# Attention recurrence, expert mixture and gated FFN on one core: the whole recurrence in a written order, experts after it, two blocks per expert, routing in two halves of twelve tiles

## The chip, the cores and the metric

One core of a Trainium2 chip runs the whole program in one launch. The metric is the device time of one execution in microseconds (us). Engines are named as the profile names them: PE is TensorE's matmuls, PEld its weight loads, DVE VectorE, ACT ScalarE, POOL GpSimd, SP SyncE (which here issues DMAs).

## The reference

Three stages follow one another. In the code below the names are those of the reference, cut to what is computed.

```python
# 1. gated linear attention: 4 batches, 8 heads, 768 steps, head dimension 48
f = 1 / (1 + exp(-f_logit))
for t in range(768):
    state = f[:, :, t, :, None] * state + k[:, :, t] (outer) v[:, :, t]
    y[:, :, t] = q[:, :, t] @ state
x = y as (3072 tokens, 384)
# 2. mixture of experts: 8 experts, width 1024, two per token
noisy = x @ w_gate + log1p(exp(x @ w_noise)) * noise
top2, weights = two largest of noisy per token, softmax over the two
out[token] += weight * (relu(x[token] @ w1[e]) @ w2[e])
# 3. gated FFN, width 1536
xn = out / sqrt(mean(out**2) + 1e-6) * rms_g
result = (silu(xn @ w_gate2) * (xn @ w_val2)) @ w_out2
```

## The kernel before

**Recurrence.** The 768 steps of a batch are cut into 6 chunks of 128 tokens, which gives 24 chunks (NT) for the four batches; a chunk holds all eight heads. Chunk n goes through a row of helpers: clip, gates and sums turn the gate logits into running sums, prep makes the scaled keys KT and queries QT from them, keys turns KT around on PE, scores multiplies KT by QT (16 small matmuls) and masks them into AM, inter multiplies QT by the state Ss, state makes the chunk's own contribution from Ks and Vs, carry adds it to the state (su on DVE, then Ss on POOL), attend multiplies AM by Vs, and rows (one chunk later) turns the result to token rows, writes them to DRAM (xd) and makes the logits for routing (lg). The loop over chunks in gla_stream calls these helpers; chunk i's iteration also does parts of the chunks i+1 to i+5.

**Routing.** router is a generator of steps: top-2 of a set of tiles, a prefix count (PE), slot numbers, one-hot tables, and at the end a list of token rows for each expert. It runs twice: over the first NTA = 8 tiles while the recurrence runs (ahead), and over the other 16 as jobs among the first expert units (rest). After the second, experts are ranked by their count, and the late blocks go by rank.

**Experts.** An expert's tokens are cut into blocks. The first block of each expert holds CAPA = 256 rows from the first NTA tiles; then each rank has two late blocks, of 256 rows and of what CAPS leaves (256 to 348 rows). A block has 8 units of 128 hidden columns. A unit is a first product (l1: 3 slices of the input, three matmuls each), a relu that splits the result into hhi (ACT) and hlo (DVE), and, two units later, a second product (l2: three matmuls per tile of 128 rows). Every operand is split in a high and a low half, so a product is three matmuls: the function three. Block rows are gathered by GpSimd DMAs (fetch), turned on DVE and split (turn).

**Weights.** They come as 768 KB loads on SP's queue (raw), and each holds two parts. take_part makes one part ready: ACT copies its high half (whi), another engine subtracts (wlo). FFN weights (wide parts) also need the integer operations cv on DVE. A part goes to a spot that has come free, starts the next load if there is room, and take_part is called once per unit; among the expert units a wide part is let through only every third unit (rest).

**Order.** PE's order is as written throughout. In the recurrence up to chunk 14 (FETCH + 3) the order of ACT, DVE and POOL is as written too (manual_schedule(ALL)); afterwards a scheduler sets theirs. From chunk 14 on, the driver behind gla_stream takes turns between the recurrence and expert_stream by their costs (debt), so that expert products stand between the recurrence's matmuls on PE, with PSUM banks as SHARED gives them. expert_stream runs over all units of all blocks: 192 expert units, then 6 FFN blocks of 512 tokens with 12 units each.

**FFN.** A unit multiplies by gate and val (18 matmuls of 512 columns), makes sg on ACT and DVE, splits to hhi and hlo, and multiplies by out (12 matmuls of 384 columns). Its inputs are gathered, combined, normalized and turned by steps attached to the units ahead.

## Time and profile before

| | us |
|---|---|
| median of 3 runs | 1117.58 (1116.81 to 1119.4) |
| the profiled execution, whole | 1115.89 |
| its span | 1114.1 |
| recurrence, with the first half of routing | 0 to 111.5 |
| block 0 is turned | 111.5 to 118 |
| mix of recurrence and first experts | 118 to 200.3 |
| experts with the second half of routing, then experts alone | 200.3 to 345, 345 to 641 |
| FFN | 641 to 1114.1 |

The rows from the profile have these columns. A stretch: its length, then the busy us and the instructions of each engine, the granted clock of PE as a share of the full one, the busy share of the DMA engines and GB/s. A group of instructions: line, engine, operation, the tiles it writes and reads, partitions x elements, count, then busy us and mean ns of one, then the idle time of the engine just before and what ended it. A timeline row: start, length, engine, line, operation, tiles, and in brackets the idle time before and its releaser. Matmuls are pipelined, so the length of one is longer than the distance to the next.

### The profile page before, as it was taken

How to read it: one execution, taken by the hardware profiler on the slowest of the kernel's cores; microseconds unless marked ns; L12 is line 12 of the kernel's file. 1: busy time of each engine (PE TensorE's matmuls, PEld its weight loads, DVE VectorE, ACT ScalarE, POOL GpSimd, SP SyncE). 2: the span in 40 equal slices, each digit the busy share in tenths (PEclk: the TensorE clock that was granted, in tenths of full speed). 3: DMA queues.
4: the chain of work that ended last, by engine and by line, in shares of the span. 5: the costliest groups of instructions: out<-in, count | busy, mean ns of one | idle time of the engine just before them, and what ended most of it. 6: DMA issues, size and time to landing. Idle time of an engine off the chain costs nothing. (4 is left out here: it accounts for less than half of the span.)

```text
span 1114.1 us, 18967 instructions
## 1 busy us (share of the span) xinstructions
PE 1054.8 (95%) x7057; PEld 959.4 (86%) x7057; DVE 684.8 (61%) x1463; ACT 486.9 (44%) x1100; POOL 385.1 (35%) x417
## 2 busy tenths in 40 slices
PE   5988799978889999999999999899999999999997
PEld 4877699868889999999998988788888888888886
DVE  6899775699777654565666769735345444353332
ACT  5675664545556543454554545423223223232211
POOL 2257544567674344444636443120030020110000
PEclk7987899999999999999999999999999999999999
DMA  9986444456667533444443444020020110110000
GB/s 307 296 264 217 133 156 138 136 173 202 216 211 230 184 106 104 150 142 128 156 147 121 150 129 137 33 71 15 1 85 1 37 49 1 57 29 1 29 1 31
DMA packets 87992, 132.97 MB, mean 119 GB/s; under 512 B 8719, under 2 KB 63907, under 8 KB 87891
## 3 DMA queue, kind: packets, MB, share of 16 engines
q1 hardware_dynamic: 78323, 112.25, 31.0%
q0 software_dynamic: 9568, 19.43, 6.2%
q8 instruction: 57, 0.93, 0.3%
q14 instruction: 44, 0.36, 0.1%
HBM read 107.63 MB, written 24.02 MB: 118 GB/s over the span
## 5 line engine op out<-in xcount | busy, mean ns | idle before, releaser
L655 PE MATMUL bank<-xhi,whi 128*128 128x256 f32 (+8 forms) x1008 | 340.4, 338 | 22.6 <-DVE hlo L760 14.6
L655 PE MATMUL bank<-xlo,whi 128*128 128x256 f32 (+8 forms) x1008 | 336.4, 334 | 1.2 <-DVE xlo L643 1.2
L655 PE MATMUL bank<-xhi,wlo 128*128 128x256 f32 (+8 forms) x1008 | 336.2, 333 | 0.0
L655 PE MATMUL bank<-whi,hhi 128*128 128x384 f32 (+2 forms) x728 | 247.2, 340 | 5.9 <-ACT y L776 5.9
L655 PE MATMUL bank<-whi,hlo 128*128 128x384 f32 (+2 forms) x728 | 246.0, 338 | 0.0
L655 PE MATMUL bank<-wlo,hhi 128*128 128x384 f32 (+2 forms) x728 | 245.3, 337 | 0.0
L655 PEld LDWEIGHTS bank<-xhi,whi 128*128 128x128 f32 x1008 | 191.6, 190 | 48.4 <-DVE hlo L760 17.7
L655 PEld LDWEIGHTS bank<-xlo,whi 128*128 128x128 f32 x1008 | 191.6, 190 | 17.9 <-DVE xlo L643 2.4
L655 PEld LDWEIGHTS bank<-xhi,wlo 128*128 128x128 f32 x1008 | 191.6, 190 | 17.4
L731 POOL DMA_INDIRECT xg<-xd,stokr x139 | 135.1, 972 | 141.8 <-ACT hhi L759 113.9
L760 DVE SCALAR_TENSOR_TENSOR hlo<-bank,hhi 128x256 fp32r<-128x256 f32 (+7 forms) x192 | 82.8, 432 | 110.2 <-ACT hhi L759 109.7
L210 ACT ACTIVATE whi<-raw 128x256 fp32r<-128x256 f32 (+1 forms) x320 | 127.0, 452 | 46.0 <-DMA raw<-in_moe_w_dram 37.8
L212 DVE TENSOR_TENSOR wlo<-raw,whi 128x256 fp32r<-128x256 f32 (+1 forms) x246 | 131.4, 566 | 22.7 <-ACT whi L210 22.2
L655 PEld LDWEIGHTS bank<-whi,hhi 128*128 128x128 f32 (+2 forms) x728 | 133.6, 184 | 10.1 <-ACT y L776 6.5
L655 PEld LDWEIGHTS bank<-wlo,hhi 128*128 128x128 f32 (+2 forms) x728 | 133.5, 183 | 6.2
L655 PEld LDWEIGHTS bank<-whi,hlo 128*128 128x128 f32 (+2 forms) x728 | 133.0, 183 | 3.4
L759 ACT ACTIVATE hhi<-bank 128x256 fp32r<-128x256 f32 (+7 forms) x192 | 74.8, 390 | 133.9 <-PE bank L655 131.2
L801 POOL DMA_INDIRECT xg<-yd,slots x40 | 44.0, 1100 | 243.1 <-ACT hhi L853 207.5
L850 DVE TENSOR_TENSOR sg<-bank,sg 128x512 f32<-128x512 f32 x72 | 49.7, 690 | 119.6 <-ACT sg L849 119.6
L849 ACT ACTIVATE sg<-bank 128x512 f32<-128x512 f32 x72 | 43.2, 600 | 145.4 <-PE bank L655 145.4
L853 ACT ACTIVATE hhi<-sg 128x512 fp32r<-128x512 f32 x72 | 45.4, 631 | 116.2 <-DVE sg L851 116.0
L212 POOL TENSOR_TENSOR wlo<-raw,whi 128x384 fp32r<-128x384 f32 (+1 forms) x74 | 69.5, 946 | 54.6 <-ACT whi L210 46.1
(159 smaller groups left out, 1141.3 us busy)
## 6 DMA issues: line engine op xcount, KB each, us to landing
raw<-in_moe_w_dram SPq DMA_DIRECT2D x64, 768.0 KB
Qs<-in_kq_dram SPq DMA_DIRECT2D x11, 1024.0 KB
yd<-y SPq DMA_DIRECT2D x48, 192.0 KB
Fs<-in_f_logit_dram SPq DMA_DIRECT2D x11, 512.0 KB
Vs<-in_v_dram SPq DMA_DIRECT2D x24, 192.0 KB
xd<-x SPq DMA_DIRECT2D x24, 192.0 KB
raw<-in_moe_w_gate_dram SPq DMA_DIRECT2D x6, 768.0 KB
raw<-in_moe_w_val_dram SPq DMA_DIRECT2D x6, 768.0 KB
```

What stands on the lines that cost most here:

```text
L210: nc.scalar.activation(hi[:, j], raw[:, j], AF.Copy)
L212: e.tensor_tensor(lo[:, j], raw[:, j], hi[:, j].bitcast(F32), op=OP.subtract)
L655: nc.tensor.matmul(o, a, b, start=start and i == 0, stop=stop and i == 2)
L731: paced(nc.gpsimd.indirect_dma_start(out=b.xg[i][:, k_], out_offset=None, in_=table, in_offset=bass.IndirectOffsetOnAxis(ap=rows_of[:, k_, ...
L759: mark[0] = nc.scalar.activation(hhi[:, :N], p[:, :N], AF.Relu).ins
L760: mark[1] = nc.vector.scalar_tensor_tensor(hlo[:, :N], p[:, :N], 0.0, hhi[:, :N].bitcast(F32), op0=OP.max, op1=OP.subtract).ins
L801: paced(nc.gpsimd.indirect_dma_start(out=y, out_offset=None, in_=ya if n < GROUP else yd, in_offset=bass.IndirectOffsetOnAxis(ap=at_, axis ...
L849: nc.scalar.activation(sg, ps[0], AF.Sigmoid)
L850: nc.vector.tensor_tensor(sg, ps[0], sg, op=OP.mult)
L853: mark[0] = nc.scalar.activation(hhi, sg, AF.Copy).ins
```

## The change

The recurrence, all 24 chunks, goes into the written order for all engines, and the experts start when it is over. The loop body no longer yields costs; SHARED, the debt and RATIO go. In chunk 0 the warm-up matmuls (warm) grow by 6, 4 and 6, and its attend comes before the gates of later chunks. From the sixth chunk on, clip is a Relu with bias on ACT instead of a max on DVE, and gates takes the shift back in its bias. The second operation of carry goes from POOL to DVE, and so do all wlo subtractions of expert weights that POOL had. The first routing half has 12 tiles in chunks 12 to 20, the gathers of block 0 are spread over chunks 20 to 24, and its three turns come after the recurrence. The first expert loads start at chunks 14 and 16 (2 and 4 before); take_part runs in chunks 20 to 23 (6 to 11 before).

CAPA is 384, and each rank has one late block with the rest (384 to 476 rows), so 128 expert units where 192 were. A gather has no wait on carry any more (st["C"]), up to two gathers are placed at a unit, and a block's turns are placed at 5 to 2 units ahead. In every fourth unit take_part is called twice. Input tiles are 512 wide for all blocks, and a block's second y goes through DVE in the first blocks too.

```diff
-    NTA = 8
+    NTA = 12
     GROUP = 4
-    CAPA = 256
+    CAPA = 384
...
     def constants():
         nc.vector.memset(ones, 1.0)
+        nc.vector.memset(shift, GATES_MAX + 1.5)
...
             else:
                 for j in range(shape[1]):
                     nc.scalar.activation(hi[:, j], raw[:, j], AF.Copy)
-                    e = nc.vector if banks[0] is not BANK and (j or self.late) else nc.gpsimd
-                    e.tensor_tensor(lo[:, j], raw[:, j], hi[:, j].bitcast(F32), op=OP.subtract)
+                    nc.vector.tensor_tensor(lo[:, j], raw[:, j], hi[:, j].bitcast(F32), op=OP.subtract)
...
-    def clip(n, s=slice(0, HP)):
+    def clip(n, s=slice(0, HP), scalar=True):
         f = st["f", n][:, s]
-        nc.vector.tensor_scalar(f, f, -GATES_MAX - 1.5, None, op0=OP.max)
+        st["shift", n] = scalar
+        if scalar:
+            nc.scalar.activation(f, f, AF.Relu, bias=shift)
+        else:
+            nc.vector.tensor_scalar(f, f, -GATES_MAX - 1.5, None, op0=OP.max)
     def gates(n, s=slice(0, HP)):
...
-        nc.scalar.activation(l, f, AF.Exp, scale=-1.0)
+        nc.scalar.activation(l, f, AF.Exp, scale=-1.0, bias=shift if st["shift", n] else 0.0)
...
             nc.vector.tensor_tensor(t, u, Ss[c % 2][:, :, :D], op=OP.add)
-            st["C"] = nc.gpsimd.tensor_tensor(sn, t, w, op=OP.mult).ins
+            nc.vector.tensor_tensor(sn, t, w, op=OP.mult)
...
-            with tc.issue_after(st["C"]):
-                paced(nc.gpsimd.indirect_dma_start(
+            paced(nc.gpsimd.indirect_dma_start(
...
-            with behind(), tc.high_priority(0 if banks[0] is not SHARED else 50):
+            with behind():
                 nc.vector.transpose(t[:, :, :n],
...
-                if i % 2 and t0:
+                if i % 2:
                     nc.vector.tensor_copy(y[:r], b.acc[i][:r])
...
     for r, most in enumerate(CAPS):
-        blocks += [moe_block(r, CAPA // P, 256, E + r),
-                   moe_block(r, CAPA // P + 2, most - CAPA - 256, E + r)]
+        blocks += [moe_block(r, CAPA // P, most - CAPA, E + r)]
...
-        if i < E:
-            where = (-4, -3)
-        elif i < NM:
-            where = (-5, -3, -2)
+        if i < NM:
+            where = (-5, -4, -3, -2)
...
-        while room.get(at_unit, 0) > (at_unit % 3 == 0):
+        while room.get(at_unit, 0) > 1:
...
             take_part(g_)
+            if g_ % 4 == 1:
+                take_part(g_)
...
-        for i in range(NT + 3):
-            es = ExitStack()
-            if i < FETCH + 3:
-                es.enter_context(tc.manual_schedule(engines=ALL))
...
+            for i in range(NT + 2):
...
+                if valid(i):
+                    scores(i)
+                safe()
+                if i == 0:
+                    warm(6)
+                    run(prep, 1)
...
+                if i == 0:
+                    warm(4)
+                if valid(i):
+                    state(i)
+                    carry(i)
+                    if i == 0:
+                        attend(i)
+                if i == 0:
+                    warm(6)
+                    run(decay, 2)
+                    clip(3, scalar=False)
+                    gates(3)
...
+                if i in (14, 16):
+                    start_loads()
...
+                if 20 <= i < 24:
+                    take_part(0)
...
+    plan = {12: [idle, step, step], 13: [idle, step], 14: [step, step], 15: [step], 16: [step],
+            17: [step], 18: [step], 19: [idle, step], 20: [step]}
+    for i, fn in enumerate([fn for fns in blocks[0].fetches for fn in fns]):
+        plan.setdefault(20 + (i + 1) // 3, []).append(fn)
...
-    recurrence, experts = gla_stream(), expert_stream()
-    debt, begun = 0.0, 0
-    for cost in recurrence:
...
+    gla_stream()
     gla.close()
...
+    for fn in blocks[0].turns:
+        fn()
...
-    for gap in (0, 0, 0, 0, 0, 1, 0, 0, 0, 0, 0, 0, 0, 0, 2, 1, 2, 2):
+    for gap in (0, 0, 0, 0, 1, 0, 0, 0, 0, 0, 0, 2, 1, 2, 2):
         jobs += [step] + [idle] * gap
```

Three places show how instructions stand on their engines. The first is VectorE in the recurrence: one chunk from one AM to the next, while no routing runs. AM is the masked scores, KT and QT the scaled keys and queries, lg the logits, su and Ss the state's carry, cs the gates' running sums, Fs the clipped logits. Before:

```order
L394 TENSOR_TENSOR AM<-scores,mask 128x1024
L364 SCALAR_TENSOR_TENSOR KT<-Ek,Qs_136 128x512
L456 TENSOR_REDUCE lg<-bank_789 128x16
L369 TENSOR_TENSOR QT<-cs,Qs_136 128x512
L418 TENSOR_TENSOR su<-bank_809,Ss_131 128x192
L342 SCALAR_TENSOR_TENSOR cs<-chain,L 128x512
L328 TENSOR_SCALAR Fs_132<-Fs_132 128x4x128
```

After, the same stretch:

```order
L395 TENSOR_TENSOR AM<-scores,mask 128x1024
L365 SCALAR_TENSOR_TENSOR KT<-Ek,Qs_138 128x512
L457 TENSOR_REDUCE lg<-bank_845 128x16
L370 TENSOR_TENSOR QT<-cs,Qs_138 128x512
L419 TENSOR_TENSOR su<-bank_865,Ss_131 128x192
L420 TENSOR_TENSOR Ss_132<-su,cs 128x4x48
L343 SCALAR_TENSOR_TENSOR cs<-chain,L 128x512
```

The clip (L328) has gone from VectorE, and the second operation of the carry (L420, to Ss) has come, right behind su.

The second place is TensorE at the end of the recurrence. Before, the rows around one chunk's scores, with the experts' first products (xhi, whi) and second products (whi, hhi) between the recurrence's matmuls:

```order
L655 MATMUL bank_1670<-whi_1044,hhi 128x384
L655 MATMUL bank_1670<-wlo_1045,hhi 128x384
L655 MATMUL bank_1670<-whi_1044,hlo 128x384
L430 MATMUL bank_1728<-QT,Ss_130 64x128 x8
L405 MATMUL bank_1739<-Vs_126,Ks_124 64x48 x8
L440 MATMUL bank_1728<-AM,Vs_126 64x128 x8
L390 MATMUL scores<-QT,KT 128x128 x8
L655 MATMUL bank_1795<-xhi_1465,whi_1159 128x256
L655 MATMUL bank_1795<-xlo_1466,whi_1159 128x256
L655 MATMUL bank_1795<-xhi_1465,wlo_1160 128x256
```

After, the last two chunks and what follows:

```order
L391 MATMUL scores<-QT,KT 128x128 x8
L453 MATMUL bank_1934<-columns,yT 128x112 x4
L431 MATMUL bank_1943<-QT,Ss_131 64x128 x8
L406 MATMUL bank_1953<-Vs_129,Ks_125 64x48 x8
L441 MATMUL bank_1943<-AM,Vs_129 64x128 x8
L391 MATMUL scores<-QT,KT 128x128 x8
L453 MATMUL bank_1995<-columns,yT 128x112 x4
L431 MATMUL bank_2004<-QT,Ss_132 64x128 x8
L441 MATMUL bank_2004<-AM,Vs_130 64x128 x8
L453 MATMUL bank_2034<-columns,yT 128x112 x4
L656 MATMUL bank_2078<-xhi,whi_1835 128x384
L656 MATMUL bank_2078<-xlo,whi_1835 128x384
```

No expert matmul stands before the last rows (L453) any more, and the first one is that of a block with 384 rows.

The third place is VectorE at the first units of the FFN. sg and hlo belong to the units, cv to FFN weights. Before:

```order
L850 TENSOR_TENSOR sg<-bank_8341,sg 128x512
L851 TENSOR_TENSOR sg<-bank_8351,sg 128x512
L854 TENSOR_TENSOR hlo<-sg,hhi 128x512
L850 TENSOR_TENSOR sg<-bank_8375,sg 128x512
L851 TENSOR_TENSOR sg<-bank_8385,sg 128x512
L774 COPY y<-bank_8174 128x384
L854 TENSOR_TENSOR hlo<-sg,hhi 128x512
L850 TENSOR_TENSOR sg<-bank_8419,sg 128x512
L851 TENSOR_TENSOR sg<-bank_8429,sg 128x512
```

After:

```order
L849 TENSOR_TENSOR sg<-bank_7303,sg 128x512
L850 TENSOR_TENSOR sg<-bank_7313,sg 128x512
L853 TENSOR_TENSOR hlo<-sg,hhi 128x512
L178 TENSOR_SCALAR cv<-cv 128x384 x2
L179 SCALAR_TENSOR_TENSOR cv<-raw,cv 128x384 x2
L181 SCALAR_TENSOR_TENSOR cv<-raw,cv 128x384 x2
L849 TENSOR_TENSOR sg<-bank_7356,sg 128x512
L850 TENSOR_TENSOR sg<-bank_7366,sg 128x512
L773 COPY y<-bank_7112 128x384
L853 TENSOR_TENSOR hlo<-sg,hhi 128x512
```

Between the first and the second FFN unit there is now the conversion of a weight part (cv), where none stood; counted over the whole engine, 5 of the 18 FFN parts are converted ahead of the first FFN unit, 10 before.

## Rows read from the trace of the kernel before

**Rows 1.** Stretches: us, busy us (and count) of each engine, PEclk, DMA, GB/s.

```profile
33.00:66.00 33.00, 33.00 (x490) 29.14 (x488) 29.86 (x45) 25.32 (x53) 11.99 (x17) 1.00 0.91 301
66.00:98.00 32.00, 24.44 (x254) 20.93 (x253) 30.56 (x81) 18.09 (x40) 16.37 (x17) 0.68 0.59 181
111.50:118.00 6.50, 0.89 (x16) 0.69 (x14) 5.13 (x8) 3.94 (x8) 2.07 (x3) 0.74 0.49 170
118.00:200.30 82.30, 80.66 (x859) 73.89 (x859) 55.96 (x96) 46.64 (x107) 39.19 (x48) 0.96 0.42 136
200.30:345.00 144.70, 125.32 (x878) 119.18 (x877) 119.37 (x287) 79.13 (x217) 95.13 (x96) 0.98 0.62 199
345.00:641.00 296.00, 292.90 (x1968) 280.91 (x1967) 181.82 (x440) 142.45 (x367) 139.69 (x137) 1.00 0.45 142
```

**Rows 2.** Timeline of TensorE, recurrence alone, 37 to 67 us.

```profile
37.15 1.16 PE L390 MATMUL scores<-QT,KT 48*128 48x128 f32 x16
...
63.24 1.09 PE L430 MATMUL bank<-QT,Ss 48*64 48x128 f32 x16
...
65.75 1.16 PE L390 MATMUL scores<-QT,KT 48*128 48x128 f32 x16
```

**Rows 3.** TensorE's groups by form, the mix, 118 to 200.3 us.

```profile
L655 PE MATMUL bank<-xhi,whi 128*128 128x256 f32 x51 | 16.6, 326 | 6.8 <-ACT xhi L642 5.6 <-DVE hlo L760 1.1
...
L655 PE MATMUL bank<-whi,hhi 128*128 128x384 f32 x30 | 11.2, 374 | 0.0
```

**Rows 4.** Timeline of TensorE among the experts, 377 to 381 us.

```profile
377.78 0.28 PE L655 MATMUL bank<-xhi,whi 128*128 128x256 f32 x1
...
378.85 0.34 PE L655 MATMUL bank<-whi,hhi 128*128 128x384 f32 x1
...
379.90 0.28 PE L655 MATMUL bank<-xhi,whi 128*128 128x256 f32 x1
```

**Rows 5.** Timeline of TensorE while eight tiles are routed, 66 to 98 us.

```profile
77.14 1.97 PE L430 MATMUL bank<-QT,Ss 48*64 48x128 f32 x16 [0.27 <-POOL Ss L419]
...
84.72 1.89 PE L452 MATMUL bank<-columns,yT 128*128 128x112 f32 x8
...
96.11 1.86 PE L390 MATMUL scores<-QT,KT 48*128 48x128 f32 x16
```

**Rows 6.** VectorE's groups by form, recurrence alone, 30 to 66 us.

```profile
L328 DVE TENSOR_SCALAR Fs<-Fs 128x512 f32<-128x512 f32 x7 | 4.4, 624 | 0.0
...
L418 DVE TENSOR_TENSOR su<-bank,Ss 128x192 f32<-128x192 f32 x5 | 1.8, 352 | 2.3 <-PE bank L405 2.3
```

**Rows 7.** Waits, 200.3 to 345 us: engine, waited for, total us, times, longest.

```profile
ACT whi L210 <- DMA raw<-in_moe_w_dram: 35.1, 21, 3.5
...
PE bank L655 <- DVE hlo L760: 13.4, 12, 2.0
```

**Rows 8.** The page's costliest groups: the experts' subtractions on GpSimd.

```profile
L212 POOL TENSOR_TENSOR wlo<-raw,whi 128x384 fp32r<-128x384 f32 (+1 forms) x74 | 69.5, 946 | 54.6 <-ACT whi L210 46.1
```

**Rows 9.** Timelines of GpSimd, VectorE and TensorE, FFN's first block, 658 to 701 us.

```profile
671.99 1.85 POOL L207 TENSOR_TENSOR wlo<-cv,whi 128x768 fp32r<-128x768 f32 x1 [2.82 <-ACT whi L206]
...
659.98 0.69 DVE L854 TENSOR_TENSOR hlo<-sg,hhi 128x512 fp32r<-128x512 f32 x1 [0.70 <-ACT hhi L853]
...
663.49 0.68 DVE L850 TENSOR_TENSOR sg<-bank,sg 128x512 f32<-128x512 f32 x1
...
672.65 1.73 DVE L854 TENSOR_TENSOR hlo<-sg,hhi 128x512 fp32r<-128x512 f32 x1 [0.70 <-ACT hhi L853]
...
691.77 0.67 DVE L850 TENSOR_TENSOR sg<-bank,sg 128x512 f32<-128x512 f32 x1
...
700.29 0.33 PE L173 MATMUL bank<-ident,xm 128*128 128x128 f32 x1 [2.28 <-ACT xm L824]
```

**Rows 10.** VectorE's groups by form, whole span: FFN weight slices.

```profile
L182 DVE SCALAR_TENSOR_TENSOR cv<-raw,cv 128x256 int32<-128x256 int32 x36 | 14.5, 415 | 0.1
```

**Rows 11.** Timeline of SyncE's DMA issues, 205 to 260 us.

```profile
205.22 20.39 SPq L256 DMA_DIRECT2D raw<-in_moe_w_dram  x4
```

## What I expect of the change, and how it is worked out

> **What bounds the kernel now.** I read the table of stretches first [rows 1]: from 345 to 641 us TensorE is busy for 292.9 of 296 us at the full clock, so that stage can only change through the matmuls themselves. The loss lies ahead of it. From 66 to 98 us TensorE is busy 24.4 of 32 us at a mean granted clock of 0.68 while VectorE is busy 30.6; from 200.3 to 345 us TensorE stands still for 19 us and VectorE is busy 119 of 145. From 33 to 66 us the recurrence runs alone with TensorE at 33.0 of 33 us: alone, and undisturbed, it is bound by TensorE, not by its chain. Its pace: six chunks (one head sequence) from the scores at 37.15 to those at 65.75, 28.6 us, or 4.77 a chunk [rows 2]. Mixing expert work into it can therefore fill nothing in such a stretch. From 118 to 200.3 the mix is nearly dense (80.7 of 82.3), but it holds one product after the other: 17 units of the first product and 15 of the second (51 and 30 matmuls of each kind, three and two a unit) [rows 3].
>
> A unit of 256 rows takes 1.07 us for nine 256-column matmuls and 1.05 for six 384-column ones [rows 4]: 119 and 175 ns each, 0.44 ns a further column. So by 200.3 us the old kernel has the whole recurrence and 17 x 1.07 + 15 x 1.05 = 33.9 us of expert work. Without the latter it stands at 166.4: that is what the new order has to beat.
>
> **The change, part by part.**
>
> *Recurrence alone.* Start: the fourth scores stand at 37.15 us before [rows 2]; three chunks of 4.77 are 14.3, so 22.9 us are start. The warm-up matmuls in chunk 0 stand where TensorE waits, and chunk 0's attend comes ahead of the next chunks' gates; what they can give is the low clock of the first two chunks. At the low level sixteen matmuls of a chunk take 1.97 us where 1.09 stands at the full one [rows 2, 5]. I take 6 us, between 0 and 9: fourth scores at 31.2. Then 21 chunks at 4.77, 100.2: 131.4 without routing.
>
> The clip moves from VectorE (0.62 us a chunk) to ScalarE, and the second operation of the carry comes from GpSimd to VectorE (I take the 0.35 of its neighbour of the same width) [rows 6]. VectorE is busy 29.9 us in 33, or 6.9 chunks: 4.3 a chunk, then 4.3 - 0.62 + 0.35 = 4.05. ScalarE goes from 25.3/6.9 = 3.7 to about 4.3 [rows 1]. Both stay under 4.77, so these two cost nothing while TensorE is the cover; if that went, VectorE's 4.05 would be the floor, not a loss.
>
> *First routing half, now 12 tiles, in chunks 12 to 20.* Eight tiles cost this: scores at 65.75 and 96.11 [rows 2, 5] are three chunks in 30.4 us, 16 more than 14.3. In the stretch VectorE's 30.6 less three chunks (13) leaves 17.6, of which the two wlo operations are 2 and the rest routing, slowed by GpSimd. For 12 tiles, half more of what goes by tiles and no GpSimd beside it: 17. Spread over nine chunks, VectorE needs 9 x 4.05 + 17 = 53.5 against TensorE's 43: 10.5 more. To that come the clock and the ordered waits of TensorE on routing results: the matmuls at 77.14 to 86.61 stand back to back, and all are at the low level [rows 5]. Two such chunks cost 2 x 3.8; I take 17 more in all, between 8 and 35. The recurrence ends at 148 and 1.5 us for the last rows: 150.
>
> The Trainium skill (TensorE: Matmul & The Clock Gate, "What's actually happening") says that the clock is held low by default and activity releases it. By that, chunks without gaps would come back at once, and the 17 would be 10.5. The row disagrees: 9.5 us of back-to-back matmuls, still low. The sum goes by the row.
>
> *Turning block 0.* Before, TensorE works 0.9 of 6.5 us at 111.5 to 118 [rows 1]. Now three tiles instead of two, but the first one's transpose stands inside chunk 21 in VectorE's order. Same 6 us, plus 1.5 for a slow first unit: the experts begin at 157.5, against 166.4. Gain 9.
>
> *Blocks.* First products: early 64 units of 9 x 175 ns + 9 x 175 = 3.15 us, 201.6. Late: 3348 columns over the eight experts, a block's mean of 418 columns takes 8 x 119 + 0.44 x 1300 = 1.52 us over the eight, x 9 matmuls x 8 units = 109.7; second products, 31 row tiles x 3 x 175 ns x 8 = 130. In all 441. Before, 128 units of 2.12, then 77 + 97: 445. Row tiles are the same number (7 an expert, 6 for the last), so only 576 matmuls less: gain 4.
>
> *Standing still in the experts.* Before: 641 - 200.3 = 440.7, less the 445 - 34 = 411 of products and 1.5 of routing: 28 us. Its waits are TensorE on hlo (13.4 us), behind ScalarE waiting for weights (35.1 us) [rows 7]: both are in-order engines, and a unit of 2.1 us wanted a part of weights each. Now a unit is 3.15 us for one part, the double-buffered bank of the first product leaves 4.7 us instead of 3.2, routing has 12 tiles for 16, and the 74 subtractions of GpSimd (69.5 us) [rows 8] go to VectorE, which is faster at them when GpSimd is silent: beside the GpSimd subtraction at 671.99, the same VectorE operation takes 1.73 us, and 0.69 without [rows 9]. VectorE in the first 24 units (75 us): hlo 0.5, parts 1.25 x 1.0, turns 0.45 a unit, which is 2.2 x 24 = 53, and 19 of routing: 72. That is close to full, so I leave 12 us (4 to 28). Four late row tiles on three y buffers are in that. Gain 16.
>
> *FFN weights.* Late blocks of the new kernel are 64 units for the same 64 parts, where 128 units were; a wide part is let through only every third unit. VectorE's order has 5 of the 18 FFN parts ahead of the first FFN unit, and 10 before. Thirteen are left for the first FFN block. A gate or val part is three slices with three operations each, the dearer of 0.415 us [rows 10], so 2.6 to 3.7. Before, with one part a unit, the sg operations at 663.49 and 691.77 are four units apart: 7.07 us a unit, where TensorE needs 18 x 0.23 (512 columns, 0.44 ns each above 119) + 12 x 0.175 = 6.2; the debt came due as 2.3 us ahead of the transposes at 700.29 [rows 9]. Five more parts are 13 to 18 us more for VectorE, of which about half found slack at 641 to 666. I add 8 (0 to 20). Rest of the FFN (before 1114.1 - 641 = 473) unchanged: 481.
>
> *Sum.* 157.5 + 441 + 1.5 + 12 + 481 = 1093 of span, 21 to 22 less than 1114.1. The profiled execution took 1115.9, the median is 1117.6; so 1117.6 - 21.6 = 1096.
>
> **Rivals.**
>
> *A. The expert stage keeps its waits.* Loads came some 5 us apart while ScalarE waited for them (four in 20.4 us on SP's queue [rows 11]), and the new kernel, taking 1.25 parts a unit, asks for one each 5.0 us until its 18 slots are full. If the 28 us stay: 1112. For it: the 35 us of waits. Against it: the surplus quarter isn't needed by the product, one part a unit is.
>
> *B. The clock stays low from chunk 12 on (slower).* Nothing but the recurrence is on TensorE, and each wait on routing can drop it. A low chunk is 4.77 x 1.97/1.09 or about 8.6 us. Twelve low chunks cost 46 and hide the 17 of routing: 1096 + 29 = 1125. It decides from about ten low chunks on. For it: the mean clock of 0.68 from 66 to 98. Against it: by 98 the clock was back, with chunks as dense as before. [...]
>
> *C. The FFN's weights come late.* The last val part is taken one unit ahead of its use; if each of the last five stops TensorE, 20 us rather than 8: 1108.
>
> *D. It is better than that.* The clock recovers, routing costs only VectorE's 10, the expert stage waits 4 us: 1096 - 7 - 8 - 3 = 1078.
>
> **How the numbers follow.** Forecast 0.55 (own range 1083 to 1107), A 0.15, B 0.12, C 0.08, D 0.10. The likeliest is 1096. For 8 in 10 the range reaches D's middle and A and C: low 1075, high 1119; B beyond it stays out. Measurement can tell about 0.2% (2.2 us), so faster is below 1115.3: all of D, nearly all of the forecast, most of C and three quarters of A, 0.82. Same 0.05, out of A and B's edge; slower 0.13, B and the far ends of A and C.
>
> **What would show it.** Right: scores 4.8 us apart in chunks 2 to 11; VectorE close to full in chunks 12 to 20 and 55 to 65 us there; the first 384-column matmul of block 0 at 150 to 165; standing still under 15 us from there to the FFN; first FFN matmul about 610; over 5 us more lost in the first FFN block than before. Wrong: chunks above 5.5 us without routing (then the chain, not TensorE, bounds the recurrence alone), the clock low past chunk 20, TensorE still waiting on hlo for 20 us among the early experts, or a FFN block 0 that costs nothing more.

## The result and the profile after

The changed kernel takes 1106.02 us (median of 4 runs, 1105.08 to 1109.45) against 1118.49 for the kernel before on the same chip: a ratio of 0.9893, interval 0.9865 to 0.9922. It is 12.5 us faster; the forecast was 21.6 faster, at 1096, in a range of 1075 to 1119. Beside later experiments it was run again, unaltered (e5 below): 1096.41 against 1116.47, 0.9828 (0.9802 to 0.9855). Both values are results. Between the two profiles lie 10.9 us of span, and 7.5 of them come from the stall described below.

The profile of the first (its execution took 1109.45, its span is 1107.7), in stretches, with the columns of [rows 1]: recurrence alone, routing, two places of standing still, the experts with the second routing half, the experts alone, and the first FFN block.

```profile
36.46:83.40 46.94, 46.94 (x690) 41.57 (x689) 41.76 (x63) 41.23 (x77) 2.67 (x10) 1.00 0.81 265
83.40:133.80 50.40, 41.57 (x616) 35.98 (x614) 48.39 (x124) 33.66 (x64) 4.23 (x8) 1.00 0.44 140
138.00:149.00 11.00, 4.46 (x35) 3.04 (x32) 2.42 (x6) 0.81 (x3) 8.29 (x9) 0.66 0.20 55
161.70:166.50 4.80, 0.08 (x2) 0.04 (x1) 3.08 (x7) 1.95 (x4) 0.00 (x0) 0.88 0.68 203
166.50:345.00 178.50, 174.81 (x997) 170.86 (x998) 130.54 (x358) 97.01 (x250) 88.89 (x85) 0.97 0.62 201
345.00:619.10 274.10, 272.30 (x1514) 257.43 (x1513) 162.18 (x378) 129.21 (x314) 121.45 (x119) 1.00 0.49 154
619.10:715.80 96.70, 82.91 (x369) 70.25 (x368) 77.71 (x169) 47.88 (x106) 35.52 (x21) 0.91 0.36 113
```

What to read here, row by row. Alone, the recurrence is TensorE without a gap, as in the first of [rows 1]. While 12 tiles are routed, VectorE is busy 48.39 of 50.40 us and the clock is full (1.00; 0.68 in the second of [rows 1]). In the third row TensorE works 4.46 of 11 us and nothing but GpSimd is busy: a stall that the trace of before has nothing like. The experts wait far less (175 of 178.5, where [rows 1] have 125 of 145). The last row, the first FFN block, is 96.7 us long with VectorE busy 78; before it was 79.2, from its first 512-column matmul at 643.89 to that of the second block.

The waits tell the same. TensorE waits 0.8 us for hlo among the first experts, 166.5 to 345 us, where it was 13.4 us in [rows 7]. ScalarE still waits 28.9 us for weights, where it was 35.1:

```profile
ACT whi L208 <- DMA raw<-in_moe_w_dram: 28.9, 18, 3.7
...
PE bank L656 <- DVE hlo L759: 0.8, 2, 0.4
```

And in the first FFN block, 619 to 716 us, a wait that before had none of:

```profile
POOL wlo L205 <- ACT whi L204: 51.4, 12, 11.1
ACT whi L204 <- DVE cv L181: 26.8, 22, 3.1
...
PE bank L656 <- POOL wlo L205: 10.6, 3, 3.8
```

Read from the bottom up it is a chain: TensorE waits for an FFN part's low half on GpSimd, GpSimd for ScalarE's high half, ScalarE for VectorE's cv.

The stall at chunk 22, in TensorE's timeline, 136 to 162 us:

```profile
137.38 0.67 PE L406 MATMUL bank<-Vs,Ks 128*64 128x48 f32 x16
137.88 0.43 PE L441 MATMUL bank<-AM,Vs 128*64 128x128 f32 x4
...
139.36 0.44 PE L441 MATMUL bank<-AM,Vs 128*64 128x128 f32 x4 [0.34 <-issue]
...
141.64 2.04 PE L391 MATMUL scores<-QT,KT 48*128 48x128 f32 x10 [0.17 <-issue]
148.84 2.05 PE L453 MATMUL bank<-columns,yT 128*128 128x112 f32 x8 [5.16 <-issue]
...
155.31 1.16 PE L391 MATMUL scores<-QT,KT 48*128 48x128 f32 x16
```

and what VectorE, ScalarE and GpSimd do in it:

```profile
143.12 0.36 DVE L419 TENSOR_TENSOR su<-bank,Ss 128x192 f32<-128x192 f32 x1 [1.62 <-remote]
...
147.64 0.94 POOL L730 DMA_INDIRECT xg<-xd,stoka  x1 [0.30 <-issue]
148.19 0.60 ACT L446 ACTIVATE yT<-bank 128x512 f32<-128x512 f32 x1 [10.55 <-remote]
```

An attend (L441) that takes 1.06 us in other chunks comes in handfuls, and what it releases comes later still: VectorE's su at 143.12 though its matmuls (L406) stand at 137.4, ScalarE's yT at 148.19 though the attend stands before 140.6. Low clock goes with it (2.04 us for ten matmuls of the scores). From chunk 21's scores to the last rows it takes 27.9 us here and 20.4 in e5, which has no such stall: 7.5 us more.

### The profile page after: what moved, and what is told of

The parts are those of the page before. It is cut to its first block, busy times and chain, and to the rows that moved or that the text cites. A ratio compares the mean times of both kernels' runs of the same rounds, so it can differ in the third digit from the quotient of the medians.

```text
span 1107.7 us, 17452 instructions
## 1 busy us (share of the span) xinstructions
PE 1049.3 (95%) x6497; PEld 950.0 (86%) x6497; DVE 665.5 (60%) x1475; ACT 484.6 (44%) x1048; POOL 307.1 (28%) x327
## 4 chain that ended last, share of the span: by engine, by line
PE 76%; DVE 9%; issue 6%; DMA 4%; ACT 2%; POOL 1%; SPq 1%; POOLq 0%; DVEq 0%; ACTq 0%
PE bank L656 68%; DMA raw<-in_moe_w_dram 3%; PE bank L441 2%; PE scores L391 1%; PE bank L453 1%; PE bank L431 1%; PE bank L172 1%; DVE wlo L209 1%; PE bank L406 1%; DVE cv L179 1%; DVE AM L395 1%; DVE cv L181 1%; POOL wlo L205 1%; DVE cs L343 1%; DVE KT L365 1%
## 5 line engine op out<-in xcount | busy, mean ns | idle before, releaser
L656 PE MATMUL bank<-xhi,wlo 128*128 128x512 f32 (+8 forms) x816 | 305.0, 374 | 11.7 <-POOL wlo L205 10.6
L656 PE MATMUL bank<-xhi,whi 128*128 128x512 f32 (+8 forms) x816 | 305.7, 375 | 6.6 <-ACT xhi L643 4.7
L656 PE MATMUL bank<-xlo,whi 128*128 128x512 f32 (+8 forms) x816 | 304.0, 373 | 0.0
L656 PE MATMUL bank<-whi,hhi 128*128 128x384 f32 x728 | 245.6, 337 | 2.3 <-ACT y L775 0.9
L656 PE MATMUL bank<-whi,hlo 128*128 128x384 f32 x728 | 245.7, 337 | 0.9 <-issue 0.9
L656 PE MATMUL bank<-wlo,hhi 128*128 128x384 f32 x728 | 245.3, 337 | 0.4 <-issue 0.4
L656 PEld LDWEIGHTS bank<-xlo,whi 128*128 128x128 f32 x816 | 155.3, 190 | 16.8 <-DVE xlo L644 0.3
L208 ACT ACTIVATE whi<-raw 128x256 fp32r<-128x256 f32 (+1 forms) x320 | 126.3, 451 | 32.2 <-DMA raw<-in_moe_w_dram 28.9
L656 PEld LDWEIGHTS bank<-whi,hhi 128*128 128x128 f32 x728 | 133.7, 184 | 7.6 <-DVE y L773 1.5
L656 PEld LDWEIGHTS bank<-wlo,hhi 128*128 128x128 f32 x728 | 133.3, 183 | 7.7 <-issue 1.0
L656 PEld LDWEIGHTS bank<-whi,hlo 128*128 128x128 f32 x728 | 133.3, 183 | 4.6 <-issue 1.2
L730 POOL DMA_INDIRECT xg<-xd,stoka x96 | 100.4, 1045 | 112.7 <-ACT hhi L758 77.0
```

What stands on the lines that cost most here:

```text
L208: nc.scalar.activation(hi[:, j], raw[:, j], AF.Copy)
L656: nc.tensor.matmul(o, a, b, start=start and i == 0, stop=stop and i == 2)
L730: paced(nc.gpsimd.indirect_dma_start(out=b.xg[i][:, k_], out_offset=None, in_=table, in_offset=bass.IndirectOffsetOnAxis(ap=rows_of[:, k_, ...
```

## The experiments

Each experiment is the changed kernel with the edit shown. They ran in three sittings of four kernels, each beside the kernel before (1116.06, 1116.47 and 1120.47 us), so a time is to be compared within its sitting, and the stages of the traces anywhere.

| run | us | ratio to before | last rows end | experts (first expert to first FFN product) | first FFN block |
|---|---|---|---|---|---|
| changed kernel | 1106.0 | 0.9893 | 161.7 | 452.7 | 96.7 |
| e1 gathers behind the carry | 1096.1 | 0.9846 | 150.5 | 451.5 | 96.0 |
| e2 FFN parts every 2nd unit | 1094.8 | 0.9785 | 156.7 | 451.4 | 89.1 |
| e3 clip on VectorE | 1097.7 | 0.9855 | 155.8 | 446.3 | 95.9 |
| e4 subtractions on GpSimd | 1115.0 | 0.9989 | 154.9 | 461.1 | 96.0 |
| e5 unaltered again | 1096.4 | 0.9828 | 152.5 | 451.4 | 95.9 |
| e6 no added warm-up | 1099.7 | 0.9846 | 157.3 | 443.7 | 96.6 |
| e7 FFN parts every unit | 1098.4 | 0.9842 | 155.3 | 462.3 | 80.7 |
| e8 blocks of before | 1130.4 | 1.0118 | 156.7 | 496.5 | 83.5 |
| e9 first turn later | 1108.7 | 0.9900 | 161.6 | 453.1 | 95.9 |
| e10 e9 + e2 + two xt | 1099.0 | 0.9825 | 159.3 | 451.4 | 89.6 |
| e11 e10, parts at 2 of 3 units | 1104.5 | 0.9873 | 157.4 | 458.1 | 87.6 |
| e12 carry on GpSimd | 1107.8 | 0.9876 | 154.2 | 454.5 | 100.5 |

The ratios have intervals of 0.2 to 0.5% a side, so two kernels of a sitting that differ by less than 5 us aren't told apart by their times. The stages differ from profile to profile too: the experts take 443.7 to 454.5 us in the kernels whose edits don't touch them (the changed kernel, e1, e3, e5, e6, e9, e12).

### e1 and e5: is the stall the kernel's?

```diff
-            nc.vector.tensor_tensor(sn, t, w, op=OP.mult)
+            st["C"] = nc.vector.tensor_tensor(sn, t, w, op=OP.mult).ins
...
+            with tc.issue_after(st["C"]):
                 paced(nc.gpsimd.indirect_dma_start(
...
```

> The changed kernel, with the gathers ordered behind the carry of the chunk again (the wait that the change removed); nothing else differs. In the changed kernel's trace TensorE stands almost still from 138 to 149 us, while GpSimd issues eight gathers in one unbroken series (138.5 to 148.6). Theory: the unbroken series of gathers holds TensorE up, so spacing them by the carry removes some 6 to 10 us: 1096 to 1100 us, last rows of the recurrence at 151 to 153 us instead of 161.7. Rival: the stall is an accident of the one profiled execution (its time was 1109.45, the other three 1105.1 to 1106.6): then 1105 to 1107 us as without the wait.

> The changed kernel, unaltered, beside the next three on one chip. Theory: the stall of TensorE from 138 to 149 us in its first profile is an accident, since three variants without the carry's wait (e2, e3, e4) don't show it: 1095 to 1103 us, next to e1 (1096.1) and e3 (1097.7), and the last rows at 150 to 157 us. Rival: it belongs to the kernel and the carry's wait cures it: 1104 to 1108 us, the stall again around chunk 22.

e1 gave 1096.1, as its theory had it, and this was worth nothing: the unaltered kernel (e5) gave 1096.4 in the next sitting, and none of the eight profiles of the first two sittings shows the stall, whatever the gathers wait for. In the last sitting all four kernels show it: e9, e10 and e11 at the same chunk, e12 at the last one:

```profile
152.13 2.05 PE L453 MATMUL bank<-columns,yT 128*128 128x112 f32 x8 [4.50 <-ACT yT L446]
```

In e12 the carry divides GpSimd's gathers into series of three, three and five: so it doesn't take one unbroken series, and the theory of e1 isn't supported. Three things are common to the five profiles with the stall. It begins while block 0's gathers run. The late yT comes within 2 us of the end of the last gather (148.19 and 148.58 us in the changed kernel), though the same gathers run without a stall in the other eight. And records are missing (of TensorE's 525 semaphore updates 497 to 501 are there; in the other eight none is missing). It isn't the one profiled execution: all four of the changed kernel took 1105 us or more. It isn't the chip alone either: the sitting of e5 and that of e9 ran on the same one. Whatever sets it on belongs to the sitting and not to the program alone; why the kernel before loses only 2 to 4 us in such a sitting and this one 10 stays open, and e1 was not tried in one.

### e3 and e12: what bounds the chunks with routing

```diff
-    def clip(n, s=slice(0, HP), scalar=True):
+    def clip(n, s=slice(0, HP), scalar=False):
```

> The changed kernel, with the clip on VectorE again in all chunks. Theory: VectorE bounds the chunks with routing (12 to 20) and TensorE the others: nine times 0.62 us, 5 to 6 us longer, all of it in chunks 12 to 20, and chunks 3 to 11 as before at 4.7 to 4.8 us: 1110 to 1113 us. Rival: the routing chunks are bound by the chain of waits between engines, not by VectorE's work: 1105 to 1108 us.

```diff
-            nc.vector.tensor_tensor(sn, t, w, op=OP.mult)
+            nc.gpsimd.tensor_tensor(sn, t, w, op=OP.mult)
```

> The changed kernel with the second operation of the carry on GpSimd again. My forecast costed its move to VectorE at nothing outside routing (TensorE is the cover) and at 0.35 us a chunk where VectorE is full. By that chunks 3 to 12 stay at 4.05 to 5.07 us, and chunks 13 to 20 get 0.3 us shorter each, 2 to 3 us in all: last rows at 149 to 151 where the fourth scores stand at 34.7. Rival: the hand-over to GpSimd and back is on the chain and costs more than VectorE's 0.35: chunks longer by 0.2 us or more, the whole 2 to 5 us longer.

The same eight chunks with routing (chunk 13's scores to chunk 21's) in e3, e5 and e12, with the columns of [rows 1]:

```profile
84.59:136.98 52.39, 41.65 (x615) 36.03 (x613) 50.64 (x131) 28.68 (x57) 5.52 (x8) 1.00 0.42 131
```
```profile
81.69:132.07 50.38, 41.56 (x615) 35.98 (x613) 48.37 (x124) 33.68 (x64) 4.21 (x8) 1.00 0.43 137
```
```profile
81.32:130.16 48.84, 41.25 (x616) 35.75 (x614) 46.78 (x119) 33.75 (x64) 11.12 (x14) 1.00 0.43 138
```

VectorE's busy time is 50.64, 48.37 and 46.78 us, and each stretch is 1.8 to 2.1 us longer than that: VectorE bounds this stage, and what is put on it or taken off (2.27 and 1.59 us) comes out nearly whole (2.01 and 1.54 us). In the stretch without routing all three take 46.94 us: there TensorE covers it. Both sizes were off. e12 takes off five operations and not eight, as the first and the last chunk of a sequence have no such operation. e3's clip takes

```profile
L329 DVE TENSOR_SCALAR Fs<-Fs 128x512 f32<-128x512 f32 x7 | 2.8, 399 | 0.0
```

0.40 us here, with GpSimd busy for 5.5 of 52.4 us, and 0.62 in [rows 6], where GpSimd was busy for 12 of 33. So seven clips are 2.8 us and not 5 to 6. The whole times, 1097.7 and 1096.4, are too close to show it. e12's first FFN block takes 100.5 us, 4 to 5 more than the others with this pacing; its edit doesn't touch that block, and no run shows why.

### e4 and e8: what took the experts' waits away

```diff
-                    nc.vector.tensor_tensor(lo[:, j], raw[:, j], hi[:, j].bitcast(F32), op=OP.subtract)
+                    e = nc.vector if banks[0] is not BANK and (j or self.load.rank is not None) else nc.gpsimd
+                    e.tensor_tensor(lo[:, j], raw[:, j], hi[:, j].bitcast(F32), op=OP.subtract)
```

> The changed kernel, with GpSimd again doing the subtractions that it did before (all of the early experts' parts prepared inside the recurrence, and the first slice of each later one of the early experts). Theory: the move to VectorE is what took TensorE's waits for hlo away (13.4 us before in 200 to 345 us, 0.8 now in 160 to 345): 8 to 14 us longer, 1113 to 1120 us, with waits for hlo back. Rival: the longer units of 384 rows did it, 1104 to 1108 us.

```diff
-    CAPA = 384
+    CAPA = 256
...
-        blocks += [moe_block(r, CAPA // P, most - CAPA, E + r)]
+        blocks += [moe_block(r, CAPA // P, 256, E + r),
+                   moe_block(r, CAPA // P + 2, most - CAPA - 256, E + r)]
```

> The changed kernel with the blocks of before: 256 rows early and two late blocks per rank, the first half of routing still of 12 tiles, the subtractions still on VectorE. It also converts 27 slices ahead of the FFN, so the experts are read apart, from the first expert product to the first FFN product (452 us in the changed kernel, products alone 441). Theory: the longer units of 384 rows give ScalarE and VectorE time for the weights, a third of the 16 us that I put on standing still, and 4 us are the 576 matmuls saved: 458 to 466 us. Rival: VectorE's subtractions did all of it: 455 to 457 us.

The waits of TensorE on hlo and of ScalarE on weights, e4, 163.7 to 345 us (the last row is the one wait for block 0, before its first product):

```profile
ACT whi L208 <- DMA raw<-in_moe_w_dram: 48.1, 23, 7.3
...
PE bank L657 <- DVE hlo L760: 9.0, 7, 3.8
PE bank L657 <- ACT xhi L644: 8.9, 1, 8.9
```

and e8, 159 to 345 us:

```profile
ACT whi L208 <- DMA raw<-in_moe_w_dram: 35.0, 25, 4.2
...
PE bank L656 <- DVE hlo L759: 16.6, 12, 2.9
```

Both halves of the change are needed, and the rivals, one cause alone, both fell. With the subtractions on GpSimd the experts take 9.7 us longer than in e5 (461.1, and 6.6 more than the longest of the kernels whose edits don't touch them), and block 0 starts 8.9 us after the last rows instead of 4.7, since its gathers queue behind subtractions on GpSimd. As a whole, e4 takes 1115.0 us where the kernel before takes 1116.1: this edit alone takes the gain back. VectorE isn't relieved by it: it is busy 132 of 181 us in this stage, in e5 136 of 188, as the subtractions that it keeps take longer beside GpSimd's. e4, then e5:

```profile
L210 DVE TENSOR_TENSOR wlo<-raw,whi 128x384 fp32r<-128x384 f32 x30 | 29.4, 985 | 12.0 <-ACT whi L208 11.9
L760 DVE SCALAR_TENSOR_TENSOR hlo<-bank,hhi 128x384 fp32r<-128x384 f32 x51 | 27.8, 546 | 7.5 <-ACT hhi L759 7.5
```
```profile
L209 DVE TENSOR_TENSOR wlo<-raw,whi 128x384 fp32r<-128x384 f32 x66 | 34.1, 548 | 7.9 <-ACT whi L208 7.8
L759 DVE SCALAR_TENSOR_TENSOR hlo<-bank,hhi 128x384 fp32r<-128x384 f32 x56 | 30.9, 552 | 14.3 <-ACT hhi L758 14.1
```

With the short units the experts take 45 us longer, of which only 4 are products. That is far beyond what I expected (458 to 466; 496.5 measured). The stretch shows most of it: from 159.6 to 345 us TensorE is busy 161 of 185 us at a clock of 0.92, and in e5 181.6 of 187.8 at 0.97:

```profile
159.60:345.00 185.40, 160.97 (x1048) 153.56 (x1049) 140.36 (x402) 103.90 (x291) 74.21 (x73) 0.92 0.66 217
```
```profile
157.20:345.00 187.80, 181.60 (x1045) 178.71 (x1046) 135.96 (x371) 100.62 (x261) 96.03 (x91) 0.97 0.62 201
```

ScalarE waits for weights about as long in both (35.0 and 37.1 us). My reading is that at 2.1 us a unit the wait reaches TensorE and at 3.15 it doesn't. Not all of the 45 us is the units' length: e8 also converts 13 more slices of FFN weights among the experts, which e11 below pays with 6.7 us there (its first FFN block is 12.4 us shorter than e5's in return). Before, 17 of the short units stood between the recurrence's matmuls, spread over 82 us; that this spared them such waits is argued and not shown. Shown is that the new order with the old blocks is slower than the kernel before (1.0118). No run has the larger blocks in the old order, so the recurrence first and the larger blocks can't be judged apart.

A rule of the Trainium skill (SBUF — State Buffer, "Who interferes with whom") bears on e4: a VectorE instruction with two inputs in SBUF contends with GpSimd's instructions that read SBUF. e4 agrees: wlo (both inputs in SBUF) takes 0.99 us there and 0.55 in e5, while the experts' hlo (bank is in PSUM) takes 0.55 in both. [rows 9] agree for the FFN's hlo, which has both inputs in SBUF (1.73 and 0.69 us).

### e6: the warm-up matmuls

```diff
-                    warm(6)
                     run(prep, 1)
...
-                if i == 0:
-                    warm(4)
...
-                    warm(6)
                     run(decay, 2)
```

> The changed kernel without the sixteen warm-up matmuls that the change added to chunk 0. My forecast gave them and the earlier attend 6 us; the traces show the fourth scores at 32.9 to 37.7 us against 37.15 before. If they lift the clock of the first chunks, the fourth scores come at 37 to 40 us without them and the whole takes 2 to 5 us longer. Rival: they take as much on TensorE as they give back: fourth scores at 32 to 36 us, the whole within 2 us.

Fourth scores at 36.74 us; with the warm-up they stand at 32.87 to 37.65 over twelve profiles, 35.2 in the mean. The start is that unsteady without any change, as the clock of the first chunks rises at different places. One profile can't tell 2 us from that; the whole times (1099.7 and 1096.4) can't either. Inconclusive, but for one thing: a gain of 6 us would have put the fourth scores near 41 us, beyond all of these.

### e2, e7, e11: the FFN's weights

```diff
-            count["rest"] = g_ + 2
+            count["rest"] = g_ + 1
```

> The changed kernel, with an FFN weight part let through every second expert unit instead of every third (22 of 48 weight slices converted ahead of the first FFN unit instead of 14). Theory: the first FFN block lost 17.5 us (96.7 us against 79.2 before) because the weights are converted there; with eight slices fewer left it takes about 87 us and the whole 1096 to 1099 us. Rival: the conversion only moves its price into the expert units, or the block waits for the loads themselves: 1104 to 1107 us.

e7 has `g_`, e11 `g_ + (1 if k_ % 2 else 0)` (with the edits of e10).

> The changed kernel with no pacing of the FFN's weight parts among the experts (38 of 48 slices converted ahead of the first FFN unit; 14 in the changed kernel, 22 in e2). Theory: each part less in the first FFN block is worth its VectorE time, 2.6 to 3.7 us, until the block has the 76 us of the later ones: block 0 at 77 to 80 us against 96, and the experts no longer, so 16 to 19 us less than the changed kernel beside it. Rival: eight parts more among the last experts delay hlo there: experts 454 to 460 us instead of 452, gain under 10 us.

> e10, but a wide part passes at two of three expert units (27 of 48 slices ahead of the FFN; e2 22, e7 38). Theory: between e2 and e7 the first FFN block falls by 2.6 us a part, and the experts rise only where VectorE gets a part at each unit, so block 0 at 84 to 86 us, the experts under 454, and 2 to 4 us less than e10. Rival: the experts pay as in e7 (462 against 451): the same as e10 or 3 us longer.

Slices converted ahead: 14 (e5), 22 (e2), 27 (e11), 38 (e7). First FFN block: 95.9, 89.1, 87.6, 80.7 us. So the first eight slices, three parts, were worth 6.8 us. VectorE is busy 77.7 us in that block in e5 and 71.1 in e2, so what was taken off came out whole: none of it had found slack. The next five slices were worth only 1.5 us. The kernel before had 27 of its 48 slices ahead too, and its block took 79.2 us where e11's takes 87.6. Before, e5 and e11:

```profile
643.90:723.10 79.20, 76.38 (x362) 66.14 (x362) 62.49 (x140) 40.00 (x84) 25.41 (x17) 0.98 0.30 95
```
```profile
608.60:704.50 95.90, 83.09 (x367) 70.31 (x366) 77.68 (x169) 47.80 (x106) 35.51 (x21) 0.93 0.36 114
```
```profile
618.70:706.30 87.60, 79.84 (x368) 67.91 (x367) 68.42 (x140) 40.27 (x85) 26.98 (x18) 0.96 0.30 97
```

With the same 140 operations VectorE is busy 5.9 us more in e11 than before. Five of its conversions (cv) fall beside a subtraction of GpSimd there and take 1.5 to 2.6 us, where the others take 0.28 to 0.55; one of them, VectorE's and GpSimd's row:

```profile
639.00 1.95 DVE L179 SCALAR_TENSOR_TENSOR cv<-raw,cv 128x256 int32<-128x256 int32 x1
```
```profile
638.79 1.87 POOL L205 TENSOR_TENSOR wlo<-cv,whi 128x768 fp32r<-128x768 f32 x1 [3.72 <-ACT whi L204]
```

In the block of before no conversion takes more than 0.6 us, in e5's three do. So a part's price isn't fixed: it depends on what GpSimd does beside it. e8 has 27 slices ahead as well, and VectorE busy for 62 us; its block is 4.3 us longer than before, with a wait of 7.2 us for the turning of the next input.

From 27 slices on, the experts pay: 458.1 (e11) and 462.3 (e7), where e2 and e10 have 451.4 and the longest of the kernels without such an edit 454.5. By time the rivals held in both: e11 takes 5.6 us longer than e10, where 2 to 4 less were expected, and e7 1098.4 us where the unaltered kernel beside it takes 1096.4. e7's waits, 560 to 645 us, show the price where it now stands:

```profile
POOL wlo L205 <- ACT whi L204: 43.3, 13, 3.9
ACT whi L204 <- DVE cv L181: 31.7, 24, 2.6
...
PE bank L656 <- DVE hlo L759: 8.9, 5, 2.7
```

A part at each unit keeps VectorE from hlo, and TensorE waits in the experts instead of the FFN. Experts and first FFN block together take 547.3 us (e5), 540.5 (e2), 545.7 (e11) and 543.0 (e7): every second unit has the smallest sum, by less than the experts of like kernels differ. e2's rest of the debt comes due at once:

```profile
PE bank L172 <- ACT xm L823: 10.2, 1, 10.2
```

(613 to 702 us): the turning of the next block's input, as at 700.29 in [rows 9], only longer.

### e9 and e10: the first turn, and all together

```diff
-            with behind():
+            es = behind()
+            if mark[0] is None:
+                es.enter_context(tc.issue_after(st["C"]))
+            with es:
                 nc.vector.transpose(t[:, :, :n],
```

with `st["C"]` set by the carry, as in e1.

> The changed kernel with one edit: the first turn of block 0 (xt) is ordered on VectorE behind the last carry instead of ahead of chunk 22's su. In e5 VectorE waits there 2.89 us for a gather, TensorE 2.26 us for Ss behind it, and 2.7 us of low clock follow: the last scores come 8.4 us after those before. Theory: that place costs 4 us; the last two scores come 4.1 to 5 us apart and the last rows at 146 to 150 us where the fourth scores stand at 34 to 35. Rival: the gathers themselves are late, and VectorE waits for them behind the carry just as long: last rows as in e5, 152 to 153. The whole 1090 to 1094 us by the one, 1095 to 1098 by the other.

> e9 together with e2's pacing (a wide part every second expert unit) and two buffers for xt instead of one. Theory: the gains add, 4 us of the turn, 7 us of the first FFN block (89 us instead of 96), 1 to 2 us of the turning of block 0 after the last rows (4.7 us now): 1083 to 1088 us. Rival: the gains are within what single executions differ by, 1092 to 1096 us.

In e5 the place that I meant is plain, in VectorE's timeline:

```profile
140.18 0.68 DVE L741 STREAM_TRANSPOSE xt<-xg 128x384 f32<-128x384 f32 x1 [2.89 <-DMA xg<-xd,stoka]
140.80 0.31 DVE L419 TENSOR_TENSOR su<-bank,Ss 128x192 f32<-128x192 f32 x1
```

e9 ran in a sitting with the stall, and it lies on that very chunk: there is no xt ahead of su any more, and su still waits 3.35 us; the view names no releaser (remote).

```profile
143.23 0.36 DVE L419 TENSOR_TENSOR su<-bank,Ss 128x192 f32<-128x192 f32 x1 [3.35 <-remote]
```

So e9 says nothing on its edit. e10 beside it does say something of the others: 1099.0 against 1108.7 (short of the 1083 to 1088 expected, as the stall is in both), with a first FFN block of 89.6 against 95.9 and 3.2 us from the last rows to the first expert product against 4.7, so both went as expected. e2 (0.9785) and e10 (0.9825, with the stall) have the lowest ratios, with the unaltered e5 (0.9828) beside them. e2 is 1.3 us faster than e1 of its sitting, which the times don't tell from nothing; e10 is 9.7 us faster than e9. The unaltered kernel itself ran in neither of these two sittings.

## Why the prediction was right, and where it wasn't

The sign and the mechanism held, and both results lie in the range. That e5 lies on the forecast is in part luck: its span is 3.8 us above the 1093 of the sum, but five terms are off by 3.5 to 7.2 us, three up and two down. Step by step, with the first profile and e5:

- **Recurrence alone.** Pace 4.77 us forecast; ten chunks in 46.94 us are 4.69. Right. The clip and the carry cost nothing there: 46.94 us in e3 and e12 too.
- **Start.** This term was mis-sized: 6 us forecast, 0.7 in the first profile, 2 in the mean. The second scores come no earlier than the 17.11 us of before: at 17.5 to 20.8 us over the twelve profiles with the added warm-up, and at 17.5 in e6 without it.
- **First routing half.** 17 us forecast, 12 measured: eight chunks take 50.4 us, and 38.2 at 4.77 each. VectorE's 10.5 of that was nearly right. What I added for the clock was wrong: it stays full, though TensorE has gaps of up to 1.6 us (a mean of 1.00 in nine of the thirteen profiles, of 0.97 in the other four). With it rival B fell. By the rule of the Trainium skill that the forecast weighed (TensorE: Matmul & The Clock Gate, "What's actually happening") the term was 10.5. The 12 us lie nearer to that than to my 17, but these rows don't test the rule: the clock did not fall, so it had nothing to come back from.
- **End of the recurrence.** 150 forecast; 152.5 in e5, 161.7 in the first profile. From chunk 21's scores to the last rows 15.8 us were forecast; e5 takes 20.4, with VectorE's wait of 2.89 us for a gather, a wait of TensorE behind it and low clock, and the first profile 27.9, with the stall. No step of mine had either. The first expert product: 157.5 forecast, 157.2 in e5, 166.5.
- **Experts.** 441 of products, 1.5 and 12 of standing still, 454.5 in all; 451.4 in e5, 452.7. Right in the sum, and rival A fell. Its parts were off against each other: TensorE stands 5.5 us and is busy 447 (6.2 and 445 in e5), part of it at low clock. That the surplus of parts did no harm is not tested by a run of its own. e8 shows that the unit's length carried it, and e4 that the subtractions did; e8's price is more than I had put on it.
- **FFN weights.** The step that failed: "about half found slack at 641 to 666". Forecast 8 us, measured 16.7 to 17.5. Five parts of 2.6 to 3.7 us are 13 to 18, and nothing of it found slack: VectorE is busy 15.2 us more in that block than before (77.7 against 62.5 in e5), and the block is 16.7 us longer. The price itself is not only that of the conversions: some fall beside GpSimd's subtractions and take three to nine times as long (e11). Part of the block's length is low clock: 0.91, 0.98 before. Rival C named the place and, at 20 us, came nearer.

For the first profile the sum is: 11.7 us late at the end of the recurrence (start 5, the last three chunks 12, routing 5 and the recurrence alone 1 to the good), 4.6 early by turning and experts, 7.5 late in the FFN: 14.6, of the 14.7 us by which its span of 1107.7 lies above the 1093 forecast. The FFN is 7.5 late and not 9.5 (17.5 against 8), as the forecast counted it from 641 us, 2.9 ahead of its first matmul at 643.89; the FFN behind the first block took 0.9 longer.

## What to carry to other kernels

When work is moved away from beside a slow stage, ask what that stage may have hidden: here the new order with the old short blocks was slower than the kernel before, and only with the larger blocks did the move pay. An operation moved to a second engine doesn't relieve the first if both then slow each other: in e4 GpSimd did 60 of the subtractions, and VectorE was as busy as without it. Where an engine is already behind in a stage, put the full price of moved work on it, not half; where it is at 60%, a job at every unit still hurts what TensorE waits for, so pacing has to be tried. And run the unaltered kernel beside the variants: without e5, e1 would have been taken for a cure.

## What the runs showed of the hardware

A TensorE stall that comes with the sitting (five of thirteen profiles of kernels in the new order), in which matmuls that need 1 us release their readers 5 to 8 us late, the last of them within 2 us of the end of GpSimd's last gather; it makes the end of the recurrence 7.5 us longer than in e5, and its cause is open. VectorE's 512-element clip is 0.40 us with GpSimd nearly idle and 0.62 where GpSimd was busy for 12 of 33 us. Its 128x384 subtraction of two SBUF tiles is 0.55 us, and 0.99 where GpSimd does part of the subtractions; the hlo of the same size, with one input in PSUM, is 0.55 in both. Its conversions of FFN weights, 0.28 to 0.55 us, took 1.5 to 2.6 beside a 128x768 subtraction of GpSimd (e11). The clock stayed at its upper level (granted clock 1.00 in nine of the thirteen profiles, a mean of 0.97 in four) through 50 us of small matmuls with gaps of up to 1.6 us between them, and it fell in the last chunks and in the first FFN block, around waits of TensorE of 2 to 5 us.
